# Two one-bank PSUM tiles for the Y and Z products of an attention and expert kernel, with a new order table

## The chip, the cores and the metric

The kernel runs on one core of one Trainium2 chip. The metric is the device time of one execution in microseconds (us), taken as the median of several runs. Engine names are those of the profile: PE is TensorE's matmul, PEld its weight load, DVE VectorE, ACT ScalarE, POOL GpSimd, SP the engine whose queue issues the DMAs.

## The reference

Three stages follow one another; all data is fp32.

```python
# attention: q, k, v of shape (2, 8, 768, 64), with hashed buckets as a mask
mask = q_bucket[:, :, :, None] == k_bucket[:, :, None, :]
scores = np.where(mask, scale * np.matmul(q, k.transpose(0, 1, 3, 2)), -1000000000.0)
attn = softmax(scores); x = np.matmul(attn, v)           # laid out as (1536, 512)
# first expert stage: w_in (512, 2048), w_out (2048, 512)
h = x @ w_in
g = np.where(h >= 1, h, np.where(h <= -1, 0.0, (h + 1) ** 2 / 4))
x = g @ w_out
# second expert stage: w_a, w_b (512, 1536), w_out (1536, 512)
out = ((x @ w_a) * (x @ w_b)) @ w_out
```

## The kernel before

The 1536 tokens are worked in four blocks of 384. The attention runs head by head; its score tiles (`qk`, line 666) are `[128, 2, 512]` fp32, two PSUM banks, from the pools `s0` and `sx`. The PSUM has eight banks: at first `s0` (2), `p` (2, one-bank tiles), `sx` (2) and `px` (2); when the first accumulator of the first expert stage is wanted, `sx` and `px` are closed and `acc` (4 banks) takes their place (`alloc`, line 323). `s0` stays open to the end of the kernel.

The first expert stage runs its first two blocks plainly (`hp` and `out` products), beside the attention. Its last two blocks share products: for each of eight pairs of feature tiles, `pi` (line 1315) and `pi2` (line 1340) make seven products of six matmuls each with sums and differences of the blocks and of the weights. A product is written to a tile of PSUM by `product` (line 1242), read by ScalarE or VectorE (`snap`, line 1256) or added by VectorE to a sum in SBUF (`plus`, line 1260, whose instruction is line 1262). In `pi` the product Y (weights `u[0]` on `b21`, in the trace `mz<-xsh` and `mz<-xsl`) goes to the second half of a two-bank tile of `s0` called `mz`, and the product Z (weights `u[2]` on `t1`, in the trace `mz<-tph` and `mz<-tpl`) to its first half. `plus(s1, Y)` is in the trace `ca<-ca,mz`; `gate`, then `split`, make of it the operands `gh` and `gl` of later `out` products. `pi2` adds `b22` into Z and reads it with `plus(s2, Z)`. There is one `mz` tile at a time, so Y of the next `pi` takes it after that last reading. X goes to tiles of `p` (`mx`).

The second expert stage does the same with `ab` (line 1265) and `ab2` (line 1284), for twelve feature tiles in each of two pairs of blocks: X in `p`, Y in the fourth bank of `acc`, Z in the first half of the one tile of `s0` (its second half is not used).

Nothing is scheduled while the kernel runs. The program lists 3686 entries, each with its reads and writes (`Program.add`), and the table `ORDER` gives the order in which they are emitted and the engine of each: a letter (p TensorE, a ScalarE, v VectorE, g GpSimd, s the DMA queue of SyncE) and the step from the entry before. Each engine works through its own entries in this order. An entry's buffer gets the slot that has been free longest (`issue`, line 249). In `Program.add` the two halves of `mz` are kept apart, as `(Z, 0)` and `(Z, 1)`; the waits in the compiled program are put in by the tile framework, from the tiles that an instruction touches.

Of the kernel before, what the change touches and what calls it, by code (L numbers as in the profile page):

```python
# [9 lines left out]
F32 = mybir.dt.float32  # L10
# [24 lines left out]
s3 s-2 v5 v p12 a2 v-16 v-3 p9 a s17 v-16 p-5 a p7 s17 s-29 a42 g v-37 p12 a p v s271 a v v v109 p-382 a a p-11  # L35
p p42 a s-47 g p33 a v p a v s-22 a-1 s5 a-3 a2 p-14 p20 v v-5 v p26 s-1 v23 g p-30 v a7 p8 s-18 p16 v g-16 a-13
s279 s-45 p-238 v a34 a p-9 a-7 g a10 p21 v v s301 v-327 p21 a g-20 g13 v8 p-11 v p21 a a243 a-277 g17 a-4 g19
p3 a g-5 s-5 g14 a10 a-23 s-12 v43 a-50 v51 p17 v p-32 p-17 p19 v-1 a2 a p-12 v-8 a s-14 g27 g-33 v28 p22 v v p
a v p-12 p26 s-1 a-102 v a62 a97 a-79 s-16 v15 g15 v-93 p66 a36 p8 v-37 s15 g a159 v-172 a50 g p-19 v p-19 v a20
a p16 v-97 a46 g19 a17 v16 v a-38 p39 a v p-30 v s-40 p33 s-3 g12 a v12 v-4 p26 p-25 v a115 v a-91 a-37 a17 v44  # L40
v68 p-91 a a-26 a22 s-6 g p33 p3 g-11 s-65 p28 v-9 v45 p-23 p9 a24 v v-33 p16 a46 s-79 g47 g-93 a98 v v-27 g-7
s-18 g27 s26 g s120 s-146 p35 v s p-34 a125 v a-140 p17 s-5 v6 a-2 a-3 a-4 g18 v114 p-92 v-63 a33 s187 v-95 p-88
v a26 a161 p-153 a a p-22 a-13 p51 p3 v-92 p265 a v-214 v38 g-51 g15 p10 v27 a2 v p-25 a18 v p14 a-49 a118 p-113
g-1 v8 v5 p7 a58 a-67 a35 s-48 p49 s-9 s-39 s25 v91 v-96 a-10 a17 g-16 g13 v-5 a30 s-23 v-4 a a22 p-4 p23 v53
v-52 s75 a-74 v145 p-149 a v-21 a g37 p-52 s30 v-29 p25 s47 v-71 v25 g-15 p44 p128 g-168 g13 s2 a26 v a-30 p25
p-7 v p24 a65 g-104 a18 g-1 p-16 a39 a-24 g14 p-3 v-5 a11 s-2 v74 v-82 p19 s-10 v-4 a v77 v17 p-79 v a-2 s83
p-77 p2 g-3 a105 a-72 v73 v-104 a21 v11 p-48 a18 a p8 a-15 s19 v7 p6 a g-32 a54 p-17 a g17 v-38 v-2 v21 p-10 s-7
v8 p43 g-50 v9 v42 p-50 v v a-7 a14 g12 p-3 v a-12 g17 a35 p-3 a p-31 s92 v-127 p76 a-40 p v a-9 a32 g-111 p84
v35 p-19 g-10 s-9 a10 v12 v66 g v-50 v-19 a-12 a89 a-51 p-6 p25 v v v-26 v57 a-73 g-55 s31 p25 a-5 a23 g-1 p4
s-18 a48 v p6 a-42 a86 g s-105 a61 v14 v-49 p29 p7 a v-7 a s-58 v25 a s68 g-64 g29 p-28 v v v-25 p90 a p-54 a v  # L50
p32 v a15 v v p-49 a33 s-53 g32 g22 s40 s-93 a94 v v a-40 g19 p-4 v a-52 a-15 a16 v a51 v a-51 v p14 a a v p16 a
s-4 p24 v g-73 p58 s44 s-53 a29 a-25 a-17 v75 v-74 s88 a-51 a29 v s-28 p17 a p-13 a v23 s-10 g-20 s2 g-23 p54 v
a-30 g p26 a p-6 p-45 p57 v a12 p-71 p2 a26 a27 v17 v s41 s-54 a-3 g20 v-48 a g a31 g p-27 a a48 p-11 v a5 a-4
p-12 a a v-25 p40 v v-15 p30 v a17 v v v-16 a-40 g25 p16 a v-3 v21 a-22 s41 a p-33 a s-31 a32 v32 v2 v-1 p-25
# [221 lines left out]
def attn_moe_kernel(ctx: ExitStack, tc: tile.TileContext, q, k, v,  # L276
# [1246 lines left out]
```

## Time and profile before

| | |
|---|---|
| median of three runs | 783.85 us (782.39 to 785.16) |
| the profiled execution | 782.08 us, of which 780.3 us are the span from the first to the last instruction |
| TensorE busy | 748.2 us, 96% of the span |
| VectorE busy | 683.9 us, 88% |
| ScalarE busy | 540.6 us, 69% |
| GpSimd busy | 362.9 us, 47% |

Three stretches follow each other: attention with the plain half of the first expert stage, to about 357 us; the `pi` stage, to about 465 us; the `ab` stage, to the end. A busy TensorE counts overlapping matmuls once, so a stretch in which it is 100% busy holds no wait longer than the part in which one matmul overlaps the next.

### The profile page before, as it was taken

How to read it: one execution, taken by the hardware profiler on the slowest of the kernel's cores; microseconds unless marked ns; L12 is line 12 of the kernel's file. 1: busy time of each engine (PE TensorE's matmuls, PEld its weight loads, DVE VectorE, ACT ScalarE, POOL GpSimd, SP SyncE). 2: the span in 40 equal slices, each digit the busy share in tenths (PEclk: the TensorE clock that was granted, in tenths of full speed). 3: DMA queues.
4: the chain of work that ended last, by engine and by line, in shares of the span. 5: the costliest groups of instructions: out<-in, count | busy, mean ns of one | idle time of the engine just before them, and what ended most of it. 6: DMA issues, size and time to landing. Idle time of an engine off the chain costs nothing.

```text
span 780.3 us, 14820 instructions
## 1 busy us (share of the span) xinstructions
PE 748.2 (96%) x5484; PEld 690.9 (89%) x5484; DVE 683.9 (88%) x1231; ACT 540.6 (69%) x1008; POOL 362.9 (47%) x318
## 2 busy tenths in 40 slices
PE   8888899999999999998989999999999999999998
PEld 5677689899989989997989999999999889999986
DVE  5999889999998988889988899999999898788764
ACT  6998899999978887787867777664546753343232
POOL 1787663635676576561412530133343237444512
PEclk9999999999999999999999999999999999999999
DMA  7999999999998878582000023443432003131011
GB/s 231 185 217 214 219 247 237 214 238 225 219 154 152 178 137 147 102 150 41 2 1 1 29 81 112 139 154 110 136 120 70 28 1 108 55 108 56 1 40 42
DMA packets 202633, 95.56 MB, mean 122 GB/s; under 512 B 165056, under 2 KB 197056, under 8 KB 202560
## 3 DMA queue, kind: packets, MB, share of 16 engines
q1 hardware_dynamic: 202272, 94.39, 52.7%
q8 instruction: 43, 0.70, 0.4%
q10 hardware_dynamic: 288, 0.22, 0.1%
q14 instruction: 30, 0.25, 0.1%
HBM read 53.69 MB, written 3.15 MB: 73 GB/s over the span
## 4 chain that ended last, share of the span: by engine, by line
PE 71%; DVE 14%; ACT 9%; DMA 3%; issue 3%; POOL 0%; SPq 0%; ACTq 0%; DVEq 0%; POOLq 0%
PE mx L1252 14%; PE acc L1403 13%; PE acc L1373 12%; PE mz L1252 8%; PE hp L1069 7%; PE s L683 6%; PE pv L756 4%; PE acc L1252 3%; DVE mn L687 2%; ACT sm L689 2%; PE kp L571 2%; DVE gl L384 1%; DMA kn<-in_k 1%; ACT t L1301 1%; PE tk L498 1%
## 5 line engine op out<-in xcount | busy, mean ns | idle before, releaser
L384 POOL TENSOR_TENSOR plo<-sm,phi 128x768 f16<-128x768 f32 x59 | 102.9, 1748 | 42.4 <-ACT phi L379 24.0
L687 DVE TENSOR_REDUCE mn<-s 128x1 f32<-128x768 f32 x96 | 91.2, 952 | 15.6 <-PE s L683 14.9
L689 ACT ACTIVATE sm<-s,mn 128x768 f32<-128x768 f32 x96 | 85.9, 897 | 25.7 <-DVE mn L687 22.6
L384 POOL TENSOR_TENSOR wlo<-F,whi 128x512 fp32r<-128x512 f32 x47 | 67.4, 1435 | 58.1 <-ACT whi L379 27.7
L1373 PE MATMUL acc<-gh,whi 128*128 128x384 f32 x200 | 70.9, 354 | 0.1
L1373 PE MATMUL acc<-gl,whi 128*128 128x384 f32 x200 | 67.5, 337 | 1.0 <-DVE gl L384 0.9
L1373 PE MATMUL acc<-gh,wlo 128*128 128x384 f32 x200 | 67.3, 336 | 0.0
L683 PE MATMUL s<-kh,qt 128*128 128x384 f32 x192 | 55.7, 371 | 2.2 <-ACT sm L689 1.6
L1403 PE MATMUL acc<-wlo,gh 128*128 128x512 f32 x144 | 56.5, 393 | 0.0
L1403 PE MATMUL acc<-whi,gl 128*128 128x512 f32 x144 | 56.4, 392 | 0.0
L1403 PE MATMUL acc<-whi,gh 128*128 128x512 f32 x144 | 56.3, 391 | 0.0
L756 PE MATMUL pv<-vc,pth 128*128 128x65 f16 (+1 forms) x1152 | 51.3, 194 | 2.1 <-DVE t L1311 0.7
L379 ACT ACTIVATE whi<-F 128x512 fp32r<-128x512 f32 x70 | 43.5, 623 | 13.1 <-PE acc L1403 11.7
L379 ACT ACTIVATE phi<-sm 128x768 f16<-128x768 f32 x60 | 50.3, 840 | 1.6 <-DMA pth<-phi 0.9
L379 ACT ACTIVATE wkh<-ws 128x512 fp32r<-128x512 f32 x56 | 34.4, 624 | 22.6 <-DVE ws L1107 14.8
L683 PE MATMUL s<-kl,q 128*128 128x384 f32 x192 | 49.6, 339 | 0.4 <-ACT kl L597 0.3
L756 PEld LDWEIGHTS <-pth 128*128 128x128 f16 x1152 | 42.0, 98 | 8.4 <-issue 7.9
L1252 PE MATMUL mz<-tph,wkh 128*128 128x384 f32 x128 | 43.7, 341 | 3.1 <-DVE ca L1262 3.1
L1252 PE MATMUL mx<-tph,wkh 128*128 128x384 f32 x128 | 44.0, 344 | 1.0 <-ACT ca L379 0.9
L1069 PE MATMUL hp<-xsh,whi 128*128 128x384 f32 x128 | 43.6, 341 | 0.7 <-DVE vs L460 0.6
L1252 PE MATMUL mx<-tph,wkl 128*128 128x384 f32 x128 | 43.2, 337 | 0.0
L1252 PE MATMUL mz<-tpl,wkh 128*128 128x384 f32 x128 | 43.1, 337 | 0.0
(279 smaller groups left out, 2510.2 us busy)
## 6 DMA issues: line engine op xcount, KB each, us to landing
stage<-in_moe_w_out SPq DMA_DIRECT2D x31, 512.0 KB, 4.3
stage<-in_moe_w_a SPq DMA_DIRECT2D x17, 512.0 KB, 3.5
stage<-in_moe_w_b SPq DMA_DIRECT2D x17, 512.0 KB, 3.5
stage<-in_moe_w_in SPq DMA_DIRECT2D x16, 512.0 KB, 4.6
kn<-in_k SPq DMA_DIRECT2D x16, 192.0 KB, 3.4
out<-ob SPq DMA_DIRECT2D x12, 256.0 KB, 2.1
vn<-in_v SPq DMA_DIRECT2D x4, 384.0 KB, 4.3
vscan<-in_v SPq DMA_DIRECT2D x4, 384.0 KB, 4.4
```

The costliest lines, as they stand in the source:

```text
L379: nc.scalar.activation(dst, src, ACTF.Copy)
L384: (nc.vector if e == "dve" else nc.gpsimd).tensor_tensor(dst, a, b, ALU.subtract)
L498: nc.tensor.transpose(s()[:, j * 128:(j + 1) * 128], src()[:, c * (J // 2) + j].rearrange("p t d -> p (t d)"), idt)
L571: nc.tensor.matmul(s()[0:NR, 0:HC], z[:, 32 - 32 * c:32 - 32 * c + NR], m, start=(i == 0), stop=(i == len(terms) - 1))
L683: nc.tensor.matmul(s()[:, i, 0:HC], x()[:, qs], t[i]()[:, 0:HC], start=(n == 0), stop=(n == 1))
L687: add({"dve": c_dve(S)}, lambda e: nc.vector.tensor_reduce(mn(), s()[:, :, 0:HC], AX.XY, ALU.min), r=[s], w=[mn])
L689: o = add({"act": c_act(S, True) + 0.093}, lambda e: nc.scalar.activation(sm().rearrange("p (c n) -> p c n", c=2), s()[:, :, 0:HC], ACTF.E ...
L756: nc.tensor.matmul(o[:, t, 0:D + 1 - i], w()[:, t, c, :], vcs[t]()[:, c, (1 - i) * D:(2 - i) * D + 1 - i], start=(n == 0), stop=(n == 3 * ...
L1069: nc.tensor.matmul(o()[:, 0:TB], a()[:, kk, :], m(), start=(n == 0), stop=(n == 3 * KD - 1))
L1252: nc.tensor.matmul(view()[:, 0:TB], a()[:, sl], m(), start=(start and n == 0), stop=(n == 5), skip_group_check=not start)
L1373: nc.tensor.matmul(ac()[:, 0:TB], a()[:, d, :], x(), start=(f == 0 and n == 0), stop=(f == F1 - 1 and n == 2))
L1403: nc.tensor.matmul(ac(), a()[:, ts], x().rearrange("p k n -> p (k n)"), start=(f == 0 and n == 0), stop=(f == F2 - 1 and n == 2))
```

## The change

- The pool `s0` is given back at the end of the attention, when the first Y or Z is wanted. Its two banks then become two pools of one one-bank tile each, `zy0` and `zy1`.
- In `pi`, Y and Z are tiles of their own and take a slot of these two each. In `ab`, Z takes one of the two; Y stays in `acc`.
- The table `ORDER` is new from its first entry. The entries are the same 3686, and so is all arithmetic.

The two tables, decoded, differ as follows. On TensorE 625 of the 950 entries have another place, 1.8 places away on average and at most 30. Of the 234 DMA issues on SyncE's queue 97 have another place among them, by 0.7 on average and at most 7. 403 entries have another engine: 100 go from ScalarE to VectorE and as many back, 100 from GpSimd to VectorE, 82 from VectorE to GpSimd, and 21 between ScalarE and GpSimd. Counted by the place among TensorE's 950 entries (the times are those of the trace before), the entries of the other engines are, before and after:

| TensorE's entries | time before, us | VectorE | ScalarE | GpSimd |
|---|---|---|---|---|
| 1 to 100 | 4.0 to 85.8 | 116, 116 | 115, 116 | 48, 49 |
| 101 to 200 | 85.8 to 168.4 | 116, 132 | 130, 124 | 33, 30 |
| 201 to 441 | 168.4 to 356.7 | 269, 260 | 275, 277 | 98, 99 |
| 442 to 570 (`pi`) | 356.7 to 463.6 | 177, 190 | 158, 160 | 30, 29 |
| 571 to 950 (`ab`) | 463.6 to the end | 519, 517 | 312, 308 | 105, 94 |

In the second of these stretches ten of the added VectorE entries are weight splits: casts `whi` from 5 to 10 and subtractions `wlo` from 4 to 9.

```diff
-        "s0": 1, "sx": 1, "px": 2, "p": 2, "acc": 1, "z": 1,
+        "s0": 1, "zy": 2, "sx": 1, "px": 2, "p": 2, "acc": 1, "z": 1,
...
+            elif b.tag == "zy":
+                scopes["s0"].close()
+                open_pools(("zy0", "zy1"), space=PSUM, side="right")
+                P["zy"] = P["zy0"]
             elif b.tag == "acc":
...
-        return P[b.tag].tile(b.shape, b.dtype, name=b.name, tag=tag)
+        return P[tag if b.tag == "zy" else b.tag].tile(b.shape, b.dtype, name=b.name, tag=tag)
...
     def ab(i, sb, f):
-        X, Y, Z = Buf("p", [128, 512], F32, "mx"), Buf("acc", [128, 512], F32, "acc3"), Buf("s0", [128, 2, 512], F32, "mz")
+        X, Y, Z = Buf("p", [128, 512], F32, "mx"), Buf("acc", [128, 512], F32, "acc3"), Buf("zy", [128, 512], F32, "mz")
...
     def pi(i, f):
-        X, Z = Buf("p", [128, 512], F32, "mx"), Buf("s0", [128, 2, 512], F32, "mz")
+        X, Y, Z = Buf("p", [128, 512], F32, "mx"), Buf("zy", [128, 512], F32, "mz"), Buf("zy", [128, 512], F32, "mz")
...
-        product((Z, 1), yv, u[0], 1, "b21", p, True)
+        product(Y, Y, u[0], 1, "b21", p, True)
         snap(s1, X, X)
-        plus(s1, (Z, 1), yv, ALU.add)
+        plus(s1, Y, Y, ALU.add)
...
-        product((Z, 0), zv, u[2], 0, "t1", p, True)
+        product(Z, zv, u[2], 0, "t1", p, True)
...
-    open_pools(("s0", "p"), space=PSUM)
+    scopes["s0"] = open_pools(("s0",), space=PSUM, side="right")
+    open_pools(("p",), space=PSUM)
```

## Rows read from the trace of the kernel before

**Rows 1.** The page's first part: busy time of each engine and its share.
```profile
PE 748.2 (96%) x5484; PEld 690.9 (89%) x5484; DVE 683.9 (88%) x1231; ACT 540.6 (69%) x1008; POOL 362.9 (47%) x318
```
**Rows 2.** Busy time by stretch: bounds, length, each engine, clock (of 1), DMA share, GB/s.
```profile
0.00:100.00 100.00, 83.47 (x796) 66.70 (x797) 84.12 (x152) 83.90 (x147) 62.04 (x61) 0.98 1.01 213
...
85.70:168.10 82.40, 77.52 (x742) 72.33 (x739) 75.44 (x125) 73.85 (x137) 42.99 (x35) 1.00 1.01 229
168.10:356.70 188.60, 185.94 (x1830) 172.62 (x1829) 168.78 (x279) 158.21 (x277) 119.69 (x97) 1.00 0.86 166
...
356.70:465.00 108.30, 101.13 (x603) 97.47 (x600) 96.16 (x188) 80.90 (x166) 33.45 (x30) 1.00 0.05 16
465.00:770.00 305.00, 304.93 (x1611) 286.71 (x1611) 269.52 (x507) 153.15 (x303) 112.48 (x103) 1.00 0.25 81
```
**Rows 3.** Waits of TensorE, 355 to 500 us: who waited for whom, total, times, longest.
```profile
PE mz L1252 <- DVE ca L1262: 3.1, 3, 2.3
...
PE xt L1191 <- DVE xn L795: 1.3, 1, 1.3
```
**Rows 4.** Order of time at 404 us: start, length, engine, line, operation, idle before, releaser.
```profile
403.72 0.34 PE L1252 MATMUL mx<-xsh,wkl 128*128 128x384 f32 x1
...
405.80 0.55 DVE L1262 TENSOR_TENSOR ca<-ca,mz 128x384 f32<-128x384 f32 x1
...
406.40 0.45 PE L1252 MATMUL mz<-tph,wkh 128*128 128x384 f32 x1 [2.34 <-DVE ca L1262]
...
406.68 0.33 PE L1252 MATMUL mz<-tpl,wkh 128*128 128x384 f32 x1
...
410.86 1.01 POOL L384 TENSOR_TENSOR gl<-ca,gh 128x384 fp32r<-128x384 f32 x1 [8.03 <-PE mx L1252]
...
414.54 0.33 PE L1373 MATMUL acc<-gl,wkh 128*128 128x384 f32 x1
```
**Rows 5.** The same view at 430 us and at 453 us.
```profile
429.42 0.34 PE L1252 MATMUL mx<-tph,wkl 128*128 128x384 f32 x1
...
429.45 0.55 DVE L1262 TENSOR_TENSOR ca<-ca,mz 128x384 f32<-128x384 f32 x1
...
430.05 0.44 PE L1252 MATMUL mz<-tph,wkh 128*128 128x384 f32 x1 [0.29 <-DVE ca L1262]
...
452.69 0.34 PE L1252 MATMUL mx<-tph,wkl 128*128 128x384 f32 x1
...
452.90 0.55 DVE L1262 TENSOR_TENSOR ca<-ca,mz 128x384 f32<-128x384 f32 x1
...
453.50 0.44 PE L1252 MATMUL mz<-tph,wkh 128*128 128x384 f32 x1 [0.47 <-DVE ca L1262]
```
**Rows 6.** The same view at 417 us, in another `pi`.
```profile
417.38 0.34 PE L1252 MATMUL mz<-xsh,wkl 128*128 128x384 f32 x1
...
417.56 0.33 PE L1252 MATMUL mz<-tph,wkh 128*128 128x384 f32 x1
...
418.89 0.54 DVE L1262 TENSOR_TENSOR ca<-ca,mz 128x384 f32<-128x384 f32 x1
```
**Rows 7.** Two stretches of the first 100 us, columns as in rows 2.
```profile
70.60:74.00 3.40, 2.17 (x12) 1.52 (x11) 3.40 (x6) 1.87 (x5) 1.39 (x3) 1.00 1.07 222
74.00:77.50 3.50, 3.50 (x42) 3.50 (x43) 2.94 (x6) 2.72 (x4) 2.65 (x3) 0.51 1.10 217
```
**Rows 8.** Groups by line and shape: count, busy us, mean ns, idle before, releasers.
```profile
L384 DVE TENSOR_TENSOR wlo<-F,whi 128x512 fp32r<-128x512 f32 x51 | 39.4, 778 | 1.1 <-ACT whi L379 0.8
...
L381 DVE CAST whi<-F 128x512 fp32r<-128x512 f32 x28 | 14.0, 499 | 1.7 <-PE hp L1069 1.0 <-PE acc L1403 0.5
...
L384 POOL TENSOR_TENSOR wlo<-F,whi 128x512 fp32r<-128x512 f32 x47 | 67.4, 1435 | 58.1 <-ACT whi L379 27.7 <-DVE whi L381 19.7 <-PE s L683 6.8
```
**Rows 9.** Order of time at 100 us, VectorE, GpSimd and TensorE.
```profile
99.65 2.37 POOL L384 TENSOR_TENSOR plo<-sm,phi 128x768 f16<-128x768 f32 x1
...
100.43 2.01 DVE L384 TENSOR_TENSOR gl<-t,gh 128x384 fp32r<-128x384 f32 x1
...
102.49 0.44 PE L1373 MATMUL acc<-gl,whi 128*128 128x384 f32 x1 [0.89 <-DVE gl L384]
```

More of the change, by code (lines that the diff above doesn't have):

```diff
@@ L40 @@
[L40 to L54, printed above, removed]
@@ L160 @@
[L160 to L164 removed]
+v5 s-2 v3 v p12 a2 s-20 v p9 a v p-5 a v p6 s280 a p-275 v276 s-269 a-6 p-6 v282 s-266 v375 p-384 p2 s-22 v42
@@ new lines @@
+v-27 v p40 p-16 p14 p-136 v-6 a411 a-410 a13 a83 v189 v v-254 p-25 v s771 s-767 s-1 p3 a-8 p13 p125 a-135 p133
+a-109 g15 p-19 a-14 s34 v48 p36 v278 a-391 a119 v148 v125 v-280 s-82 p2 v-22 v110 a-109 v20 g12 a71 a p-90 a8
+v-37 g v119 a g p-103 v a109 g a-109 v9 a a-9 p109 a g v-106 p-4 v v a23 g4 s2 s-1 g219 p-133 p p-96 v a a97 g
+p-2 p-1 v-7 v g v-134 p54 a a-2 a709 p-715 v a a11 s5 v70 v p7 p-87 v a87 a g-86 a-1 v88 a g p9 a g p-6 a-86
+a102 v-105 s2 p-5 p91 v-90 a a14 p-9 a p82 v-75 v79 v p-83 g16 p65 p17 v-11 v-86 a a17 p-6 v63 s-59 a82 a s-82
@@ new lines @@
+v-36 p46 a-56 a80 v-48 v38 a-33 a v26 g v10 v-33 v-3 v g p25 a-18 p7 a2 p-10 v2 p9 a-60 a4 a41 a p24 p27 a87
+p-78 p-37 p2 v-10 v-14 v27 a63 v-75 p23 p15 v38 a-86 a a202 v-201 a v-39 v79 v-4 a-28 a v g8 g60 v v-38 v89
+g-110 a48 a-31 a a282 v-281 a-16 g-22 v68 p-25 v-20 v56 p-51 a2 a p18 v-17 p40 p-30 p28 p-1 p-10 v-8 v v48 a-67
+g a-10 v p33 a2 v41 p-30 p37 p-1 p-46 p50 v-31 a-27 a v v a162 g-191 a178 a-143 v133 v-132 p46 p-20 g-32 p76
+a-50 v v113 a-112 v a-22 a v380 v-249 v-62 g2 p-46 p16 p25 p a6 g v-73 v132 a-107 a a170 v-169 v3 a44 a-46 v43
@@ new lines @@
+p-17 v-5 a-15 v a27 a v v30 v14 p-10 p-1 a-41 a v p14 a-13 p16 p v-26 g a26 p7 v20 a-18 v-8 p7 p10 v141 v-176
+a113 a36 v-104 a-26 a v p6 p43 a-42 v p7 v-259 v269 a-24 v v-245 a252 p41 p-15 p12 p p3 a-41 v v30 s-230 a v
+v280 v-279 v293 a-65 g-70 p62 a19 a-10 v a25 v p-18 v2 v68 a-86 a v p22 v20 g-34 p30 p s-181 a166 p a-24 p36
+v-35 s-185 v403 a-138 v139 v-138 a-66 a a206 p-201 p17 v-14 p17 v-24 p75 v-3 a-71 g65 v137 v8 g a-186 a41 v-65
+g202 p-130 p-1 p3 p10 v-78 v29 a-10 p57 v-56 a-188 p245 v-244 a188 v v-188 a227 v p13 a-284 v a343 v a-135 a92
@@ new lines @@
+g-121 p34 p p16 p-15 v24 v v-8 a p12 a2 v-24 v43 v-75 v106 v-63 p8 v2 p-13 a-15 g v18 v60 s-169 a v v v172 p-53
+a s26 a v a25 g v-25 p-32 v4 p18 v2 v-73 a65 v p-12 p28 a2 a-10 a21 v-20 v21 s-94 a v v66 v-65 g130 p-80 v82
+p-81 p27 p3 a2 g-28 a7 v s79 v-90 p63 a28 v p-60 v61 v-149 a89 p-18 v4 v9 p24 v2 a11 p2 p-37 v-29 p35 p a32 p
+g-50 v35 g p19 v6 s-22 v-25 v45 s26 a-21 a-40 v a15 v v v14 p33 v371 v a-375 p-53 v54 v v-23 a26 p2 v-56 v58
+a-33 a4 a498 p-520 v-6 g29 v-21 a5 p23 v-17 p-42 v61 a38 v g-11 g s-24 a v p-29 v-23 p63 p-4 p6 v-12 v-21 a45
@@ L165 @@
+v7 a15 p-4 v5 p-6 p7 a-11 v-27 v28 p5 p7 a3 v a-10 p5 v-4 v6 g a8 v p-4 v-46 p45 p-1 p8 p v3 v p-6 p8 p-1 a-4 v
+v-8 v a15 v p-4 p7 p-1 p-1 v-4 v a8 v v-117 v123 v a-10 s-63 v64 p5 p-2 p p6 v3 v p-3 p p5 a-11 v12 v g-12 p8
+p11 a s p-8 a s p-6 p7 a s
 """
@@ L1335, in pi @@
         snap(s3, X, X)
-        plus(s3, (Z, 0), zv, ALU.add)
+        plus(s3, Z, zv, ALU.add)
         gt[3, 2 * f + 1] = gate(None, None, s3)
@@ L1343, in pi2 @@
         product(X, X, u[1], 0, "t4", p, False)
-        product((Z, 0), zv, u[3], 1, "b22", p, False)
+        product(Z, zv, u[3], 1, "b22", p, False)
         gt[2 * f + 1] = split(gate(X, lambda: X()[:, 0:TB], None))
-        plus(s2, (Z, 0), zv, ALU.add)
+        plus(s2, Z, zv, ALU.add)
         gt[3, 2 * f] = gate(None, None, s2)
```

228 lines of the change are left out of this document (107 added, 121 removed).

## The prediction

> **What bounds the kernel now.** The first view is the page's share of busy time: TensorE 96%, VectorE 88%, ScalarE 69%, GpSimd 47% [rows 1]. TensorE bounds the kernel as a whole, and the change leaves its work alone: the same 950 entries, the same matmuls. So time can come only from TensorE's waits. The second view says where they are [rows 2]. TensorE is idle for 100.00 - 83.47 = 16.5 us in the first 100 us, for 82.40 - 77.52 = 4.9 us from 85.7 to 168.1 us, for 188.60 - 185.94 = 2.7 us from there to the end of the attention, for 108.30 - 101.13 = 7.2 us in the `pi` stage, and for 0.1 us of 305 in the `ab` stage. The third view, TensorE's waits in and around the `pi` stage [rows 3], names one that the change touches: three times, for 3.1 us together, the Z product waited for VectorE's `ca`. Two stretches have a second engine close to its bound: VectorE is busy for 75.44 of 82.40 us from 85.7 to 168.1 us, and for 96.16 of 108.30 us in the `pi` stage [rows 2].
>
> **Part 1, Y and Z as two tiles in `pi`.** In the order of time [rows 4] the Z product at 406.40 us begins 0.05 us after VectorE has finished `ca<-ca,mz` (405.80 + 0.55 = 406.35 us). That addition reads Y, in the other bank; Z needs nothing of it. The same happens at 430.05 us (VectorE done at 430.00) and at 453.50 us (done at 453.45) [rows 5]. That the products themselves need no such order is seen at 417.56 us [rows 6]: there Z follows Y's last matmul after 0.18 us, and the addition that reads Y begins only at 418.89. There the table has Z ahead of the addition, at the three waits behind it; so the wait comes of the tile that the two share, and of their order in the table. With two tiles it has no cause. Its price is the distance between the starts of two matmuls, less what it is without a wait, 0.17 us (417.38 to 417.56 is 0.18): 406.40 - 403.72 = 2.68, so 2.5 us; 430.05 - 429.42 = 0.63, so 0.45 us; 453.50 - 452.69 = 0.81, so 0.65 us. Together **3.6 us**, a little more than the 3.1 us of rows 3, since a matmul's end overlaps the next one's start.
>
> What is late next: with Z 2.5 us earlier, the sum `ca` keeps its own pace on VectorE, ScalarE and GpSimd, and the `gl` made of it ends at 410.86 + 1.01 = 411.87 us [rows 4]; the first `out` product that reads it begins at 414.54 [rows 4], so 2.7 us of slack cover it. I take all 3.6 us off. The bounds are 0 (each wait reappears behind another sum) and 3.6; a loss is excluded, since whatever a tile of its own waits for, the shared tile waited for too.
>
> **Part 2, two slots for Z in `ab`.** A second slot lets Z of the next tile begin before `plus(s2, Z)` of the one before. TensorE is busy for 304.93 of 305.00 us there [rows 2], so this frees nothing: 0 us. The cover is the mixture of products that the table puts between; the new table has 517 VectorE entries there in place of 519, so it stays.
>
> **Part 3, `s0` given back and two pools opened.** No instruction is added. The first Y already has to wait for the last readers of the score tile in `s0`, since it took the same slot. 0 us; no wait of that kind is among rows 3.
>
> **Part 4, the new table.** This is the uncertain part: 403 entries on another engine and 625 moved on TensorE, in stretches that the two-tile change does not concern. SyncE's 97 moved issues are moved by 0.7 places on average, so the transposes and the loads come to the same neighbours; I take 0 us for them. For the rest, the counts of entries times mean durations say what each stretch must hold. TensorE's entries 1 to 100: VectorE 116 entries as before, ScalarE and GpSimd one more each; no sign. Entries 201 to 441: VectorE loses 9 entries, a relief, and TensorE has 2.7 us of idle time there to give back at most. Entries 442 to 570: VectorE gains 13 entries of about 96.16 / 188 = 0.51 us, 6.6 us in all, so 102.8 of the 104.7 us that are left of the stretch after part 1: 98%, which still fits. Entries 101 to 200: VectorE gains 16 entries of 75.44 / 125 = 0.60 us, 9.7 us in all (ten of them are `whi` and `wlo`, at 499 and 778 ns, which gives 5 x 0.50 + 5 x 0.78 = 6.4 us for these [rows 8]). That makes 85.1 us in a stretch of 82.4. Either VectorE falls behind by 2.7 us and makes it up in the relieved stretch behind it, or TensorE waits. I take 0 for the likeliest case, because the next stretch has 188.60 - 168.78 = 19.8 us of free VectorE to make it up in; the bounds are -2.7 us (the idle time behind entry 200) and +9.7 us.
>
> One more term hangs on the table. From 74.0 to 77.5 us TensorE's granted clock was 0.51, the lower of its two levels (1.2 GHz), after a stretch of 3.4 us in which it was busy for 2.17 us [rows 7]. It cost at most half of 3.5 us, 1.7 us. With other waits in the first 100 us it may go or come a second time: -1.7 to +1.7 us; I take 0.
>
> **The sum.** The profiled execution took 782.08 us, 1.8 us more than its span of 780.3 and 1.77 us less than the median of 783.85. 782.08 - 3.6 = 778.5 us, and on the median **780.3 us**, 0.46% less. A measurement of this kernel can tell about 0.3%, 2.35 us, from no change.
>
> **Rivals.** *VectorE binds between TensorE's entries 101 and 200.* Place and mechanism are above: more subtractions and casts than the stretch has room for, and TensorE's `out` products stand behind `gl` and `whi` in VectorE's queue. It decides from the point at which the added 9.7 us exceed VectorE's idle time there, 82.40 - 75.44 = 7.0 us, by more than it can lag. The price is 2.7 us (VectorE without any gap) to 9.7 us (the same gaps as before), the middle 6.2; with part 1, 782.9 to 790.0 us, the middle **786.5**. For it speaks that VectorE's instructions are not always as short as their mean: at 100.43 us a `gl` took 2.01 us while GpSimd worked on a `plo` from 99.65 to 102.02, and TensorE waited 0.89 us for it [rows 9]. Against it speaks that TensorE was nearly free of waits from 168.1 us on with VectorE at 89% [rows 2]. The Trainium skill, SBUF — State Buffer, section "Who interferes with whom", says that a VectorE instruction with two SBUF inputs contends with a GpSimd instruction that reads SBUF, and that the one that comes second waits for the other to end. Rows 9 agree. By that rule each of the five added `wlo` could meet a GpSimd `wlo` of 1435 ns [rows 8], an estimate of up to 7.2 us more, and the rival would be at the upper end of its range.
>
> *The wait only moves.* The sums of the `pi` stage stand in a VectorE queue that is to be 98% full, so that other products wait where Z waited; the 3.6 us stay. That gives **783.9 us**. For it: the 13 added entries. Against it: the slack of 2.7 us at `gl`, and that TensorE waited in only three of eight `pi`.
>
> *The attention gains as well.* The relief of VectorE behind TensorE's entry 200 frees the 2.7 us of idle time there, and the fall of the clock goes, 1.7 us: 780.3 - 4.4 = **775.9 us**. For it: 9 VectorE entries fewer there. Against it: the clock's fall hangs on waits of half a microsecond that no count of entries shows.
>
> **How the numbers follow.** Forecast 0.42, with a range of its own of 777.5 to 783; VectorE binds 0.26; the wait only moves 0.18; the attention gains as well 0.14. Of the forecast three quarters lie under 781.5 us (0.32), the rest within 0.3%; the case of more gain is all faster, and 0.02 of the two other cases may be: faster 0.48. Within 0.3%: 0.10 of the forecast, 0.16 of the moved wait, and 0.05 of the bound VectorE, whose lower end is 782.9: 0.31. Slower, over 786.2 us: 0.21, nearly all of it VectorE. For 8 in 10 the range takes in the bounds of the forecast, all but 0.05 of the gain case (its spread is that of the forecast, some 2.5 us) and all but the top of the VectorE case, 0.10: 774.5 to 788.5 us.
>
> **What would show it.** Right: in the `pi` stage no wait of `mz` for `ca`, Z's first matmul in each `pi` free to begin before the addition that reads Y has ended, and TensorE's idle time from 356.7 us to the end of that stage down from 7.2 to about 4 us; the `ab` stage as long as before; TensorE's 200th entry at about 168 us. VectorE bound: TensorE's 200th entry at 171 to 178 us, with waits for `gl`, `wlo` or `whi` on VectorE before it. Moved: as many microseconds of idle time in the `pi` stage with other names. Gain: no clock of 0.51 in the first 100 us, and the attention over before 356 us. The prediction is wrong if the attention's length changes by more than 3 us either way, since part 4 is put at nothing without a row that shows it.

## The result and the profile after

The changed kernel took 776.73 us (median of four runs, 776.21 to 778.35) beside 783.74 us of the kernel before (782.39 to 785.16): a ratio of 0.9914, 95% interval 0.989 to 0.9937. Two more comparisons of the same two kernels, shown below, gave 0.9936 [0.9913, 0.9959] and 0.9917 [0.9892, 0.9942]. The three average 0.9922, so the change saves about 6.1 us; forecast were 3.6. It is faster, and more so than forecast.

The profiled execution took 776.21 us against 782.08, 5.87 us less. The page's first part for the changed kernel, which answers to [rows 1]:

```profile
PE 746.3 (96%) x5484; PEld 690.6 (89%) x5484; DVE 686.8 (89%) x1249; ACT 538.1 (69%) x1001; POOL 349.3 (45%) x305
```

TensorE has the same 5484 matmuls and nearly the same busy time; VectorE has 18 instructions more, GpSimd 13 fewer. Of the 5.9 us of span that went (780.3 to 774.4), 4.0 are TensorE's idle time (32.1 to 28.1) and 1.9 its busy time. TensorE's waits in and around the `pi` stage of the changed kernel, 350 to 500 us (columns as in [rows 3]):

```profile
PE mx L1255 <- ACT ca L382: 1.4, 1, 1.4
PE mx L1255 <- ACT cc L382: 0.9, 1, 0.9
PE mx L1255 <- DVE cc L384: 0.9, 1, 0.9
PE xt L1194 <- ACT xn L382: 0.8, 2, 0.6
PE mz L1255 <- DVE wkl L387: 0.5, 1, 0.5
PE acc L1369 <- DVE wlo L387: 0.2, 1, 0.2
```

The wait of `mz` for `ca`, 3.1 us in [rows 3], is gone. The three `mx` rows belong to X, whose tiles the change leaves alone; they come to 3.2 us, after 1.6 in the same view of the kernel before and 1.5 with two tiles and the old table (e1 below). So the new table, not the tiles, gave some of the gain back here. The order of time from 375 us shows what the two tiles allow (start, length, engine, line, operation, idle before, releaser):

```profile
375.18 0.33 PE L1255 MATMUL mz<-tph,wkh 128*128 128x384 f32 x1
...
377.80 0.34 PE L1255 MATMUL mz<-xsh,wkh 128*128 128x384 f32 x1
...
379.13 0.56 DVE L1265 TENSOR_TENSOR ca<-ca,mz 128x384 f32<-128x384 f32 x1 [1.51 <-PE mz L1255]
380.94 0.34 PE L1255 MATMUL mz<-xsh,wkh 128*128 128x384 f32 x1
...
384.29 0.55 DVE L1265 TENSOR_TENSOR cc<-cc,mz 128x384 f32<-128x384 f32 x1 [0.24 <-PE mz L1255]
```

The Z product of the second `pi` runs at 375.18 us, ahead of Y (377.80) and of the addition that reads Y (379.13). At 380.94 the next `pi`'s Y is already written, while the last reading of this one's Z comes at 384.29. Before, Y of the next `pi` had to wait for that reading; the prediction did not list this second freedom.

For a comparison by stages, this table takes the starts of TensorE's entries 100, 201, 442, 568 and 950 in each trace, and gives the differences of the lengths between them against the profiled execution before: longer (+) or shorter (-), in us. The cuts stand where both tables have done the same TensorE entries. e7 is left out, since it adds matmuls.

| version | to entry 100 | 100 to 201 | 201 to 442 | `pi`, 442 to 568 | 568 to 950 |
|---|---|---|---|---|---|
| before, length | 84.6 | 83.8 | 188.3 | 104.8 | 314.2 |
| changed kernel | +0.62 | -0.85 | -1.90 | -2.74 | -0.97 |
| e5, the same again | +5.04 | -0.79 | -0.74 | -2.75 | -0.94 |
| e11, the same a third time | -1.50 | +0.20 | -2.06 | -2.96 | -0.98 |
| e1, two tiles, old table | -0.28 | -0.30 | -0.01 | -3.45 | +0.11 |
| e2, one tile, new table | +0.99 | -0.30 | -1.92 | +3.36 | +4.97 |
| e3, new attention, old rest | +1.17 | -1.14 | -1.22 | -3.00 | +0.16 |
| e4, old attention, new rest | +2.30 | +0.11 | -0.03 | -2.63 | -0.95 |
| e6, 16 entries to VectorE | +0.21 | +10.80 | +0.04 | -2.76 | -0.97 |
| e8, two products swapped | +2.31 | -0.91 | -1.86 | -2.89 | -0.94 |
| e9, new order, old engines | +13.63 | +14.34 | +37.58 | -2.46 | -0.95 |
| e10, old order, new engines | +21.13 | +20.98 | +32.59 | -2.48 | -0.97 |

Among the three executions of the changed kernel the two last columns repeat to 0.2 us, the middle ones to 1.3; the first scatters by 6.5; the section on the clock (e5, e7, e11) comes back to it.

### The profile page after: what moved, and what is told of

Read it like the earlier page. It is cut to its first block, busy times and chain, and to the rows that moved or that the text cites. A ratio compares the mean times of both kernels' runs of the same rounds, so it can differ in the third digit from the quotient of the medians.

```text
span 774.4 us, 14809 instructions
## 1 busy us (share of the span) xinstructions
PE 746.3 (96%) x5484; PEld 690.6 (89%) x5484; DVE 686.8 (89%) x1249; ACT 538.1 (69%) x1001; POOL 349.3 (45%) x305
## 4 chain that ended last, share of the span: by engine, by line
PE 76%; DVE 13%; ACT 5%; DMA 3%; issue 2%; SPq 0%; ACTq 0%; DVEq 0%; POOL 0%
PE mx L1255 17%; PE acc L1369 14%; PE acc L1399 13%; PE mz L1255 9%; PE hp L1072 6%; PE s L686 6%; PE pv L759 4%; PE acc L1255 3%; DVE mn L690 3%; ACT sm L692 2%; PE kp L574 1%; DMA ptl<-plo 1%; DVE F L969 1%; DVE plo L387 1%; PE tq L541 1%
## 5 line engine op out<-in xcount | busy, mean ns | idle before, releaser
L387 POOL TENSOR_TENSOR plo<-sm,phi 128x768 f16<-128x768 f32 x56 | 99.5, 1784 | 36.1 <-ACT phi L382 18.7
L387 POOL TENSOR_TENSOR wlo<-F,whi 128x512 fp32r<-128x512 f32 x37 | 52.8, 1428 | 50.6 <-ACT whi L382 21.9
L382 ACT ACTIVATE whi<-F 128x512 fp32r<-128x512 f32 x73 | 45.1, 623 | 7.5 <-PE acc L1399 6.9
L387 DVE TENSOR_TENSOR wlo<-F,whi 128x512 fp32r<-128x512 f32 x61 | 47.8, 784 | 0.3
L387 POOL TENSOR_TENSOR wkl<-ws,wkh 128x512 fp32r<-128x512 f32 x18 | 27.2, 1516 | 36.0 <-ACT wkh L382 29.8
```

The costliest lines, as they stand in the source:

```text
L382: nc.scalar.activation(dst, src, ACTF.Copy)
L387: (nc.vector if e == "dve" else nc.gpsimd).tensor_tensor(dst, a, b, ALU.subtract)
```

## Experiments on the two parts: the tile and the table

**e1: two tiles with the old table.** The changed kernel with the order table of before.

```diff
 ORDER = """
-v5 s-2 v3 v p12 a2 s-20 v p9 a v p-5 a v p6 s280 a p-275 v276 s-269 a-6 p-6 v282 s-266 v375 p-384 p2 s-22 v42
+s3 s-2 v5 v p12 a2 v-16 v-3 p9 a s17 v-16 p-5 a p7 s17 s-29 a42 g v-37 p12 a p v s271 a v v v109 p-382 a a p-11
...
```

> The changed kernel with the order table of the kernel before: Y and Z have tiles of their own, and nothing else differs from before. Theory A (the tile shared by Y and Z made three waits, worth 2.5, 0.45 and 0.65 us): about 3.6 us less than before, 780 us, a ratio of 0.995, and no wait of the Z product for the sum ca in the stage of shared products. Theory B (the new table alone made the gain): within 1 us of before, 783 to 784 us, with other waits in the place of the three.

Measured: 779.78 us (778.19 to 782.13), ratio 0.9943 [0.992, 0.9966]. The `pi` stage is 3.45 us shorter, the stage behind it as long as before (+0.11). The place of [rows 4] in this kernel's order of time:

```profile
400.20 0.34 PE L1256 MATMUL mz<-xsh,wkh 128*128 128x384 f32 x1
...
402.84 0.34 PE L1256 MATMUL mz<-tph,wkh 128*128 128x384 f32 x1
...
404.77 0.55 DVE L1266 TENSOR_TENSOR ca<-ca,mz 128x384 f32<-128x384 f32 x1
```

Z begins at 402.84 us in place of 406.40 and 1.93 us before the addition that reads Y; in [rows 4] it began 0.05 us after that addition's end. With the same table, only the tile differs: the wait came of the tile that Y and Z shared, and its price was the forecast's 3.6 us within 0.2.

**e2: one tile with the new table.** Y and Z are again the halves of one two-bank tile.

```diff
-                open_pools(("zy0", "zy1"), space=PSUM, side="right")
-                P["zy"] = P["zy0"]
+                open_pools(("zy",), space=PSUM, side="right")
+                P["both"] = P["zy"].tile([128, 2, 512], F32, name="mz", tag="zy0")
...
-        return P[tag if b.tag == "zy" else b.tag].tile(b.shape, b.dtype, name=b.name, tag=tag)
+        if b.tag == "zy":
+            return P["both"][:, b.slot]
+        return P[b.tag].tile(b.shape, b.dtype, name=b.name, tag=tag)
```

> The changed kernel with its new table, but with Y and Z in the two halves of one two-bank tile that is opened once. Theory A: the waits of a product for the reading of the other half come back wherever the table puts the reading first, now for Y as well as for Z and in the last stage too; at least 3 us more than the changed kernel, 780 us or more. Theory B: as fast as the changed kernel, 776 to 778 us.

Measured: 790.2 us (788.57 to 792.33), ratio 1.0065 [1.0046, 1.0085]: slower than before. The waits of TensorE over its whole span:

```profile
PE mz L1257 <- DVE cc L1267: 4.7, 5, 1.9
...
PE mz L1257 <- DVE ca L1267: 2.1, 1, 2.1
...
PE mz L1257 <- DVE cb L1267: 1.1, 3, 0.4
```

Products wait nine times for an addition that reads this tile, 7.9 us in all: 4.1 in `pi` and 3.8 in the last stage. The changed kernel has none of these waits. The table of stages agrees: `pi` is 3.36 us longer than before and 6.1 longer than in the changed kernel, the last stage 4.97 and 5.9 longer. In `pi` a part of this is TensorE's clock, which fell in e2 and not in the changed kernel (columns as in [rows 2]):

```profile
426.70:430.10 3.40, 1.55 (x9) 1.42 (x9) 2.46 (x6) 1.14 (x2) 1.65 (x2) 1.00 0.00 0
430.10:433.50 3.40, 3.40 (x13) 3.40 (x12) 1.31 (x3) 1.64 (x4) 0.00 (x1) 0.50 0.00 0
```

At half the clock, 3.4 us cost at most 1.7 of the 6.1. So the new table leans on the two tiles: in the `ab` stage, where the second slot gained nothing with the old table (e1, +0.11), it is worth 5.9 us with the new one.

**e3 and e4: each half of the new table alone,** cut at TensorE's 442nd entry, both with two tiles. The table is the new one up to the cut and the old one behind it (e3), or the reverse (e4).

```diff
 (e3, the first line that differs)
-p-2 p-1 v-7 v g v-134 p54 a a-2 a709 p-715 v a a11 s5 v70 v p7 p-87 v a87 a g-86 a-1 v88 a g p9 a g p-6 a-86
+p-2 p-1 v-7 v g v-134 p54 a a-2 p-6 v a a11 s5 v70 v p7 p-87 v a87 a g-86 a-1 v88 a g p9 a g p-6 a-86 a102 v-105
...
```

> Two tiles; the entries of the attention (to TensorE's 441st) in the new table's order and on its engines, all others as in the table before. Theory A: the gain of e1 and that of the attention, which was 1.9 us in the profiles, add up: 783.7 - 3.6 - 1.9 = about 778 us, with TensorE's 441st entry about 2 us earlier than before. Theory B: no two-tile gain, 781.8 us. If the attention's 1.9 us are only the spread from run to run, about the time of e1.

> Two tiles; the attention in the order and on the engines of the table before, all behind TensorE's 441st entry as in the new table. Theory A: the attention is as long as before, the stage of shared products is 3.3 us shorter and the last stage 0.6 us shorter than before: about 779.5 us. If the gain lies in the attention: 782 us or more.

Measured: e3 780.68 us (775.88 to 783.32), ratio 0.9953 [0.9924, 0.9982]; e4 780.01 us (779.17 to 780.87), ratio 0.9935 [0.9912, 0.9959]. Their medians cannot be told apart, but the stages can. Between entries 201 and 442 every version with the whole of the new attention gains, 0.74 to 2.06 us in six executions, and the two with the old one gain nothing (-0.01 and -0.03). From entry 100 to 201 the six are at -1.14 to +0.20, the two at -0.30 and +0.11. So the attention gains by the table and not by the tile. Behind entry 442 the new table gives up 0.4 to 0.8 us of `pi`'s saving (-2.63 for -3.00 and -3.45) and gets 1 us in the last stage.

## Experiments on the table's attention

**e6: sixteen more entries on VectorE.** Of GpSimd's 30 entries beside TensorE's entries 101 to 200, sixteen go to VectorE; the order of the entries stays. The rival "VectorE binds" put the edge at 7 us of added work, and the change itself had added 16 entries there, so this adds as many again.

```diff
-s-3 a43 v g22 p-5 a-42 g11 a-9 p35 a6 p s-62 s93 a-30 p-33 p67 s-70 v-8 v5 a a79 v-48 g-30 a31 s64 v-90 v p12
+s-3 a43 v v22 p-5 a-42 v11 a-9 p35 a6 p s-62 s93 a-30 p-33 p67 s-70 v-8 v5 a a79 v-48 g-30 a31 s64 v-90 v p12
...
```

> The changed kernel with 16 more of GpSimd's 30 entries between TensorE's 101st and 200th entry given to VectorE, spread evenly; nothing is moved in order. Rival of the prediction (VectorE binds in this stretch once its added work exceeds its idle time): VectorE is idle for about 82.4 - 78.3 = 4.1 us there, and 16 entries of 0.6 to 0.75 us are 10 to 12 us, so 6 to 8 us more than the changed kernel, 783 us or more, lost before TensorE's 201st entry. Other theory (the entries take the place of waits and of time in which VectorE was held up by GpSimd): at most 3 us more.

Measured: 789.17 us (787.58 to 793.2), ratio 1.0078 [1.0049, 1.0106]. Busy time between the starts of TensorE's entries 101 and 201 (one entry apart the same work), before, in the changed kernel and in e6 (columns as in [rows 2]); three views:

```profile
85.80:168.40 82.60, 77.72 (x741) 72.54 (x737) 75.64 (x125) 74.08 (x136) 42.89 (x35) 1.00 1.01 230
```
```profile
86.10:168.20 82.10, 78.88 (x770) 73.49 (x770) 78.03 (x134) 71.60 (x129) 40.56 (x32) 1.00 1.09 239
```
```profile
86.30:179.40 93.10, 82.15 (x769) 75.57 (x769) 86.51 (x149) 72.14 (x127) 19.23 (x16) 0.97 0.94 206
```

In the changed kernel VectorE was busy for 78.03 us there, not the 85.1 that the prediction worked out, and the stretch is 0.5 us shorter. In e6 VectorE is at 93% over a stretch that is 11 us longer, and TensorE's waits for VectorE's `q` there are 1.9 and 1.7 us. The granted clock is 0.97 over that stretch, for at most 93.1 x 0.03 = 2.8 us of the 11. So a loss of the rival's size exists, beyond what the change added. That a full VectorE is its cause is not shown: in the changed kernel VectorE was busy for 95% of the stretch (78.03 of 82.10 us) without a loss.

**e9 and e10: the new order with the old engines, and the old order with the new engines.** Where does the attention's gain come from, the relief of VectorE or the places of the products? Both versions alter the attention alone, and keep the rest of the changed kernel. In e9 the order of entries is the new one and 227 entries have their old engine; in e10 the order is the old one and the engines are the new ones.

```diff
 (e9)
-v5 s-2 v3 v p12 a2 s-20 v p9 a v p-5 a v p6 s280 a p-275 v276 s-269 a-6 p-6 v282 s-266 v375 p-384 p2 s-22 v42
+v5 s-2 v3 v p12 a2 s-20 v p9 a v p-5 a v p6 s280 a p-275 v276 s-269 a-6 p-6 v282 s-266 v375 p-384 p2 s-22 a42
...
```

> Changed kernel, but every entry of the attention (those ahead of TensorE's 442nd entry in the old table) has the engine that the old table gave it; the order of entries is the new one throughout. So far the new table's attention was 1.2 to 2.6 us shorter than the old one's from TensorE's entry 101 to entry 442 (-1.20, -2.43, -2.44, -2.53, -2.61 against the profiled execution before, with the old table -0.33 and +0.08). Theory: the gain is VectorE's relief, nine entries fewer beside TensorE's entries 201 to 441. Then it goes here: -0.4 to +0.2 us between these entries, and the time is that of the old attention with two tiles and the new rest, 780.0 us, so 779 to 781. Rival: the gain is the new places of TensorE's products among themselves and the order of the other engines' queues. Then it stays, -2.4 us, and the time is that of the changed kernel, 776.7 to 779.1. Half of each if both matter, 778.5. The pi stage and the ab stage are to be as long as in the changed kernel in either case.

> The other half of the same split: the attention in the old order, but every entry of it on the engine of the new table (VectorE 266 entries beside TensorE's entries 201 to 441 in place of 269, and 125 beside entries 101 to 200 in place of 116); the rest is that of the changed kernel. Theory (the engines carry the gain): TensorE's entries 101 to 442 are 1.2 to 2.6 us shorter than before, time 776.7 to 779.1. Rival (the order carries it): -0.4 to +0.2 us, time 779 to 781. A third outcome, longer than before by some us, would say that these engines and that order only work together, each fitted to the other; then 781 to 784.

Measured: e9 844.21 us (843.65 to 846.72), ratio 1.0773 [1.0746, 1.0801]; e10 856.06 us (853.3 to 861.1), ratio 1.0921 [1.0889, 1.0953]. Neither theory holds. It is the third outcome that e10's text names, far beyond the 781 to 784 us given there. Between entries 101 and 442, in the changed kernel and in e9:

```profile
86.10:354.60 268.50, 263.66 (x2597) 245.16 (x2597) 242.69 (x407) 232.52 (x407) 161.28 (x130) 1.00 0.95 187
```
```profile
99.70:422.30 322.60, 280.60 (x2598) 252.20 (x2598) 251.76 (x399) 233.51 (x413) 159.17 (x131) 0.97 0.76 153
```

The engines do nearly the same work: VectorE 399 instructions in place of 407, ScalarE 413 in place of 407, GpSimd 131 in place of 130. No engine of e9 is busier than 87% of the stretch, and VectorE is at 78%, less than the changed kernel's 90%. Yet it is 54 us longer. TensorE's first wait of e9 over the whole span, and ScalarE's:

```profile
PE s L686 <- ACT sm L692: 20.0, 26, 4.0
```
```profile
ACT sm L692 <- DVE mn L690: 54.2, 47, 4.3
```

In the changed kernel these two are 3.9 us in 9 waits and 24.0 in 39. The chain from a head's scores over the row's extreme (`mn`, VectorE) and the exponential (`sm`, ScalarE) back to TensorE is late, link by link, although every engine has time. The clock is lower as well, 0.979 to 0.982 in the mean in e9 and 0.970 to 0.982 in e10; by the line of the section on the clock that is about 9 and 11 of the 60 and 72 us over the kernel before. So which engine an entry has and where it stands in the order fit each other, and the number of entries in a stretch did not tell the outcome: by number, e9 relieves VectorE beside TensorE's entries 101 to 200 (120 entries in place of 132), where e6 loads it (148), and both lose. Which of the two, the engines or the places, carries the attention's gain stays open, since neither works alone.

## Experiments on the moved wait and on the clock

**e8: two products swapped in the fifth `pi`.** The changed kernel waits 0.91 us at 414.22 us with an X product (`mx`), and its Z product stands right behind it. Here Z goes first.

```diff
-v-192 p p-2 v-23 v v270 p-232 g9 g-57 v108 g-97 p36 a-21 a a8 v-7 v163 v61 p-177 p p2 p-16 v-26 v38 a-45 v p33
+v-192 p-1 p2 v-25 v v270 p-232 g9 g-57 v108 g-97 p36 a-21 a a8 v-7 v163 v61 p-177 p p2 p-16 v-26 v38 a-45 v p33
```

> The changed kernel with one pair of TensorE's entries exchanged: in the fifth pair of feature tiles the Z product (t1) goes ahead of the product t3 that waits 0.9 us for a copy of X on VectorE. Theory A (a wait in the stage of shared products goes in full to the end of the kernel, since TensorE is busy behind it): 1.07 us less than the changed kernel in the trace between TensorE's 510th and 571st entry and at the end. Rival (the wait only moves behind another sum): no difference at the 571st entry.

Measured: 777.63 us (775.55 to 778.22), ratio 0.9912 [0.9888, 0.9936]. The order of time, first in the changed kernel, then in e8:

```profile
412.62 0.34 PE L1369 MATMUL acc<-gh,wkh 128*128 128x384 f32 x1
...
414.22 0.44 PE L1255 MATMUL mx<-tph,wkh 128*128 128x384 f32 x1 [0.91 <-DVE cc L384]
...
416.43 0.34 PE L1369 MATMUL acc<-gh,wkh 128*128 128x384 f32 x1
...
420.11 0.33 PE L1255 MATMUL mz<-tph,wkh 128*128 128x384 f32 x1
```
```profile
414.14 0.34 PE L1369 MATMUL acc<-gh,wkh 128*128 128x384 f32 x1
...
415.73 0.44 PE L1255 MATMUL mx<-tph,wkh 128*128 128x384 f32 x1
...
416.88 0.34 PE L1369 MATMUL acc<-gh,wkh 128*128 128x384 f32 x1
...
417.94 0.33 PE L1369 MATMUL acc<-gh,whi 128*128 128x384 f32 x1
418.35 0.44 PE L1369 MATMUL acc<-gl,whi 128*128 128x384 f32 x1
...
421.22 0.44 PE L1255 MATMUL mz<-tph,wkh 128*128 128x384 f32 x1
```

Ahead of this place e8 was 1.52 us behind the changed kernel (414.14 - 412.62); at the `out` product of 416.88 it is only 0.45 behind (416.88 - 416.43), so the 0.91 us and the restart behind it were saved. Then it falls back: 0.24 us at `gl` (418.35 - 417.94 is 0.41 in place of 0.17), and 1.11 behind at 421.22 (421.22 - 420.11). At entry 571 it is 1.52 behind again. The saved wait came back in pieces of at most 0.3 us, none of which the view of waits names; e8's `pi` is 0.15 us shorter than the changed kernel's in all. Why it came back, VectorE's rows say, first in the changed kernel, then in e8:

```profile
419.09 0.55 DVE L1265 TENSOR_TENSOR cc<-cc,mz 128x384 f32<-128x384 f32 x1
```
```profile
420.61 0.55 DVE L1265 TENSOR_TENSOR cc<-cc,mz 128x384 f32<-128x384 f32 x1
```

This addition is 1.52 us behind, as TensorE was before the swap. Compared one by one, the instructions of VectorE, ScalarE and GpSimd that begin between 408 and 435 us of the changed kernel are all 1.46 to 1.53 us later in e8. None of them moved with TensorE, so they set the pace here, and TensorE fell back to it. Here the rival "the wait only moves" is what happens.

**e5 and e11: the changed kernel again, and e7: matmuls ahead of six early products.** e5 and e11 alter nothing. e7 adds 20 matmuls whose results are overwritten, two to four each ahead of six products of the first 100 us, to see whether a busier TensorE keeps its clock.

```diff
+    FILL = {329: 2, 371: 3, 409: 4, 415: 4, 422: 3, 443: 4}
...
+    def fill(me, *banks):
+        for i in range(FILL.get(me, 0)):
+            nc.tensor.matmul(banks[i % len(banks)], warm.to_broadcast([128, 128]), warm.to_broadcast([128, 512]),
+                             start=True, stop=True)
...
         def mm(e):
+            fill(me, s()[:, 0], s()[:, 1])
```

> The changed kernel once more, beside the others of this group. Theory A (two tiles 3.6 us, new attention 1 to 2 us, the rest of the table 0.5 us, at an equal clock of TensorE): 776 to 778.5 us, a ratio to before of 0.991 to 0.994. If the attention's part in the first profile was chance: 780 us, a ratio of 0.995, as with two tiles and the old table.

> The changed kernel with 20 matmuls of a constant (512 columns, their result is overwritten) ahead of six products between TensorE's 80th and 107th entry, where it waited for 0.5 to 2.9 us each. Theory of the clock (the runs of one kernel differ by falls of the granted clock in the first 100 us, each about 3.4 us long and 1.2 to 1.7 us dear): mean clock 0.999 to 1.0 in nearly all runs, a spread from run to run of 2 us in place of 4 to 7, and 0 to 2 us less than the changed kernel, since at 0.21 us each the 20 cost up to 1 us outside the waits. If the falls do not hang on these waits: clocks as before and up to 4 us more.

> The changed kernel unaltered, on the same chip as the two halves, as their yardstick. The two earlier comparisons gave 776.73 us (0.9914 of the kernel before) and 779.12 us (0.9936). If the clock's falls make the difference, as a third to four falls per execution, the runs of this one again spread over 776 to 782 us and go with their mean granted clock at about 0.5 us for each 0.001, and the ratio lies between the two, 0.992 to 0.994. If the chip makes it, the time is near one of the two with a narrow spread at any clock.

Measured: e5 779.12 us (776.65 to 781.9), ratio 0.9936; e11 777.29 us (774.79 to 779.5), ratio 0.9917; e7 780.15 us (778.4 to 783.3), ratio 0.9948 [0.9924, 0.9972]. The busy time by stretch in e5, whose profiled execution was 5.7 us longer than the first one of the same kernel (780.1 against 774.4 us of span), and then the one fall in that first one, with the stretch ahead of it:

```profile
6.60:10.50 3.90, 3.73 (x14) 2.56 (x14) 2.67 (x6) 1.54 (x3) 0.00 (x0) 0.59 0.77 238
44.00:48.00 4.00, 2.94 (x10) 2.40 (x11) 3.90 (x9) 1.96 (x4) 1.72 (x3) 0.60 1.17 283
48.00:52.00 4.00, 4.00 (x46) 3.42 (x45) 1.52 (x4) 3.83 (x8) 3.55 (x2) 0.54 0.48 106
71.00:76.00 5.00, 4.50 (x30) 3.52 (x30) 3.98 (x6) 3.47 (x7) 1.84 (x2) 0.66 1.05 217
```
```profile
74.00:78.00 4.00, 2.49 (x34) 1.87 (x30) 3.93 (x8) 3.26 (x6) 2.21 (x3) 1.00 1.12 277
78.00:82.00 4.00, 3.70 (x42) 3.37 (x43) 3.10 (x5) 3.23 (x6) 2.49 (x2) 0.57 1.36 226
```

In e5 TensorE's granted clock was down near its lower level (1.2 of 2.4 GHz) in three places of the first 76 us, in the first execution in one. That is the same program. Over the eight runs of e5 the mean granted clock went from 0.998 (776.65 us) to 0.990 (781.9 us). A straight line through all 128 runs of this study, with an offset for each kernel, gives 0.49 us for each 0.001 of mean clock, with 1.0 us of scatter about it; in e11 three runs at 0.996 took 774.79, 776.58 and 778.43 us. The line does not say whether a fall costs the time or the waits that stand ahead of it. By that line, at a clock of 1 throughout, the kernel before takes 781.6 to 782.0 us (three sets), the changed kernel 775.1 to 776.2 (three sets), e1 778.3, e2 786.4, e3 777.0, e4 777.9, e8 775.2: 6.2 us for the whole change, 3.5 for the two tiles alone.

The chip does not explain the comparisons: within one chip e11 spreads over 4.7 us, and the three medians over 2.4. e7's profiled execution had the clock at 0.77 to 0.78 over the 3.4 us from 8.9, from 46.4 and from 87.4 us, and its time at a clock of 1, 777.9 us, is about 2 us above that of the changed kernel. But e7 does not answer its question. Its added matmuls write to the tile that the product behind them takes, so they wait for the same release; two of the six places in its order of time:

```profile
78.25 1.03 PE L562 MATMUL kp<-warm 128*128 128x512 bf16 x4 [0.74 <-ACT q L642]
...
85.15 1.54 PE L562 MATMUL s<-warm 128*128 128x512 bf16 x4 [2.63 <-ACT sm L704]
```

They stand behind the waits and do not fill them. What makes the clock fall in one execution and not in the next is left open.

## Why the prediction was right, and where it was short

**Part 1 was right, and near its size.** Three waits of 2.5, 0.45 and 0.65 us, 3.6 in all, were to go from `pi`. With the old table 3.45 us went (e1), with the new one 2.74 to 2.96. The slack of 2.7 us at `gl` held: in e1 that `gl` ended at 408.82 us and the first product that reads it began at 411.18, 2.4 us later. The signs named came true: no wait of `mz` for `ca`, Z free to run ahead of the addition. TensorE's idle time in the stage fell from 7.2 us [rows 2] to 4.7, where about 4 was named; the view by stretch, `pi` between the same entries before and in the changed kernel, then most of the changed kernel's `ab`:

```profile
356.70:463.60 106.90, 99.73 (x595) 96.11 (x591) 94.79 (x185) 79.53 (x162) 33.45 (x30) 1.00 0.05 16
```
```profile
354.60:458.20 103.60, 98.86 (x590) 95.85 (x587) 95.06 (x190) 78.36 (x159) 31.59 (x29) 1.00 0.06 18
458.20:760.00 301.80, 301.78 (x1602) 285.26 (x1602) 268.76 (x510) 153.88 (x306) 104.59 (x93) 1.00 0.26 82
```

VectorE was to be 98% full there, by 13 entries of 0.51 us each, 6.6 us; it is at 95.06 of 103.60 us, 92%, and was busy for 94.79 before. Five more of its instructions fall into the stage (190 for 185), and its busy time grew by 0.27 us.

**Parts 2 and 3 at nothing** were right for the old table (e1, +0.11 behind entry 568). Under the new table that stage is 0.94 to 0.98 us shorter, which no row of waits accounts for, and with one tile it would be 4.97 longer (e2). The working "TensorE is busy for 304.93 of 305.00 us, so a second slot frees nothing" holds for the table it was read from, and says nothing of a table that uses the slot.

**Part 4 at nothing was the step that failed.** The term for TensorE's entries 101 to 441 was taken as 0 between bounds of -2.7 and +9.7 us; between entries 100 and 442 it was -2.75, -1.53 and -1.86 in the three traces of the changed kernel. In two of them most of it lies behind entry 201 (-1.90 and -2.06), where the prediction saw a relief and gave it no microsecond; in e5 it is half (-0.74). Busy time from entry 201 to 442, before and in the changed kernel:

```profile
168.40:356.70 188.30, 185.64 (x1828) 172.33 (x1827) 168.49 (x279) 157.91 (x277) 119.69 (x97) 1.00 0.86 166
```
```profile
168.20:354.60 186.40, 184.78 (x1829) 171.67 (x1828) 164.66 (x274) 160.92 (x280) 120.72 (x98) 1.00 0.88 164
```

Idle time fell from 2.66 to 1.62 us and busy time by 0.86. The view of waits names nearly the same on both sides, five waits of 1.7 us before and six of 1.8 after; what went are gaps too short for that view: in the traces those under 0.15 us come to 0.98 us before and 0.17 after. VectorE has 3.8 us less to do there and ScalarE 3.0 more. In the other stretch, entries 101 to 200, the loss did not come. The step rested on counts of entries times mean durations: 16 x 0.60 us more for VectorE, so 85.1 of 82.4 us. VectorE's row (at e6) says 78.03 us, with 134 instructions in place of 125: nine more, not 16. Part of the added entries ran behind the stretch, and the added casts and subtractions came with fewer of other kinds. By groups of one line and shape, VectorE between 85.7 and 168.1 us, before and in the changed kernel:

```profile
L384 DVE TENSOR_TENSOR gl<-t,gh 128x384 fp32r<-128x384 f32 x6 | 4.7, 789 | 0.0
L384 DVE TENSOR_TENSOR wlo<-F,whi 128x512 fp32r<-128x512 f32 x4 | 2.7, 702 | 0.0
```
```profile
L387 DVE TENSOR_TENSOR wlo<-F,whi 128x512 fp32r<-128x512 f32 x8 | 7.1, 891 | 0.2
...
L387 DVE TENSOR_TENSOR gl<-t,gh 128x384 fp32r<-128x384 f32 x3 | 1.7, 550 | 0.0
```

The mean of the subtractions `wlo` rose, 891 ns in place of 702, by two of the eight: six took 0.68 to 0.69 us, one 0.99 and one 2.03. The longest, in the changed kernel's order of time:

```profile
142.50 1.85 POOL L387 TENSOR_TENSOR plo<-sm,phi 128x768 f16<-128x768 f32 x1 [1.02 <-ACT phi L382]
...
142.87 2.03 DVE L387 TENSOR_TENSOR wlo<-F,whi 128x512 fp32r<-128x512 f32 x1
```

It began while GpSimd's `plo` ran and ended 0.55 us after it (144.90 and 144.35). That agrees with the rule that the prediction took from the Trainium skill (SBUF — State Buffer, "Who interferes with whom"), that the one which comes second waits for the other to end. But few met: by the prediction's estimate each of the five added `wlo` could meet such a neighbour, for up to 7.2 us, and here all eight together cost 8 x 0.19 = 1.5 us more. Three `gl` fewer, and shorter, gave 3.0 us back. The deeper fault is that counts did not tell the outcome in this kernel, as e9 and e10 show. The averages of 0.7 and 1.8 places with which the moves were called small are over all 234 and all 950 entries; those that moved did so by 1.7 and 2.7.

**The rivals.** "VectorE binds" did not happen; e6 lost about as much as it named (10.8 us, for 2.7 to 9.7), and the edge of 7 us of added work was put too early. But e6 also parts engines from their order, as e9 and e10 do, and VectorE's share was no higher in it, so that its loss need not be VectorE's bound. "The wait only moves" did not happen to the three waits of part 1, and did to the one that e8 takes away. "The attention gains as well" was the nearest: it said 775.9 us with 2.7 us from the attention and 1.7 from the clock. The first half came in the first trace; the second did not, since the clock's fall at 74 us [rows 7] has its like at 78 us in the changed kernel. That a fall hangs on waits of half a microsecond, as the prediction has it, no run shows. The prediction named as its own refutation a change of the attention by more than 3 us. Behind entry 100 it is -2.75 at most, so a term put at nothing took all that its bound allowed. Counted from the start to entry 442 it is -2.13 in the first trace, +3.51 in e5 and -3.36 in e11: for one and the same program the first 100 us scatter by more than the test allows, so the test decides nothing.

**The rest of the distance** to the first median: 780.3 - 776.73 is 3.6 us. That median lies just under the forecast's own range of 777.5 to 783 us and nearest to the 775.9 of the last rival; the repeats at 779.12 and 777.29 lie inside that range and just under it. The profile accounts for 5.87 - 3.6 = 2.3 of it: 2.75 (attention) + 0.97 (last stage) - 0.86 (`pi`, 2.74 for 3.6) - 0.62 (first 99 entries) = 2.2. The other 1.25 us is the step from a profiled execution to a median: 1.77 us before, taken over unchanged, and 776.73 - 776.21 = 0.52 in the first four runs after. It is within the scatter of single runs: the clock's term was put at 1.7 us either way, and the runs of one program spread over 5 us (e5).

## What to carry to other kernels

Where a product waits for a reading of the other bank of its own tile, give the two a tile each, and price it by the distance between the starts of the matmuls on either side: that sum held within 0.2 us under the same order (e1). A hand-written order and its assignment of engines are one thing: price a new table as a whole, from what the stretch has left to lose and to gain; counts of instructions times their means missed by 7 us here (85.1 for 78.03). A wait that is taken from one engine counts only where the others do not set the pace (e8). And what a table does not use today (a second slot) can be worth 6 us to the next one (e2). A kernel whose clock falls at chance is compared at equal mean clock, or over many runs, before a difference of a few microseconds gets a reason.

## What the runs showed of the hardware

The granted clock of one and the same program fell to its lower level once or three times in the first 100 us of two executions, and a run of 0.998 and one of 0.990 in the mean were 5.3 us apart (e5). TensorE was busy for a part of the time ahead of a fall: for 2.49 of 4.00 us before that of the changed kernel, for 2.17 of 3.40 before that of [rows 7], and for 1.55 of 3.40 before that of e2 at 430 us. A subtraction of two SBUF tiles of 128 x 512 on VectorE took 0.68 to 0.69 us six times out of eight in the changed kernel, and 2.03 us once, when it began while GpSimd's `plo` ran.
